# P V of the group before between the first two score chunks, row sums on DVE, odd 64 weight rows as half rows: a decode step on one Trainium2 core

## The chip, the cores and the metric

One core of one Trainium2 chip runs the whole program. The metric is the time of one execution on the device in microseconds (us), as the median of several. The profile's span, from the first to the last instruction, is about 1.8 us shorter than the time of the same execution. "Fast runs" are those not over 1.5% above the fastest of the same kernel.

PE is TensorE, which multiplies matrices and writes to PSUM; DVE (VectorE) and ACT (ScalarE) do the element-wise work; SyncE issues the loads, which 16 DMA engines carry. A load has landed when the last of the 16 engines reports it done. P is the matrix of exponentials of the scores, and "P V" its product with V.

## The reference, cut to what matters

```python
B, D, H, Sk, Dh, F = 8, 576, 32, 4096, 128, 4608          # one new token per sequence
q = (x @ wq) as [B, H, 1, Dh]
p = softmax(einsum("bhqd,bhkd->bhqk", q, k_cache) * Dh ** -0.5)
a = einsum("bhqk,bhkd->bhqd", p, v_cache) as [B, 1, H * Dh] @ wo
h = gelu(layernorm(x) @ w1 + b1);  b = h @ w2 + b2          # [576, 4608] and [4608, 576]
g = sigmoid((x * gate_w).sum(-1))
out = g * a + (1 - g) * b                                     # bfloat16
```

K and V are 268 MB each and every byte is used once, so the two caches have to stream through the core; the weights add 20 MB.

## The kernel before: the parts that matter

The work is cut into 64 groups of 4 heads of one sequence. For each group one DMA brings 4 MB of K and one brings 4 MB of V. There are two buffers for each. Within a group DVE multiplies K by q in four chunks, PE adds the products up in PSUM (8 matmuls a chunk), DVE reduces them to scores, ACT takes the exponentials, and PE multiplies P by V (32 matmuls, one group later). All DMA is issued by SyncE in program order; a V load waits for the last P V matmul that reads its buffer, a K load for the last multiply.

```python
    def load_k(g):
        s = g % 2
        nK[s] += 1
        src = kv_src(A_k_cache, g)
        k_land[g] = op("sync", lambda e: e.dma_start(KB[s][:, :, :], src), [k_done.get(g - 2)], dma=(sK[s], 16 * nK[s]))

    def load_v(g):
        s = g % 2
        nV[s] += 1
        src = kv_src(A_v_cache, g)
        t = op("sync", lambda e: e.dma_start(VB[s][:, :, :], src), [v_done.get(g - 2)], dma=(sV[s], 16 * nV[s]))
        v_land[g] = [(t, 0, NTT)]
# ... cut ...
    def pv(g, part, parts):
        s = g % 2
        for land, t0, t1 in v_land[g]:
            t0, t1 = max(t0, part * NTT // parts), min(t1, (part + 1) * NTT // parts)
            for tq in range(t0 // TQ, t1 // TQ):
                j = tq % 4
                o = o_ps[s][32 * j:32 * j + TQ * HB, :]
                w = [land, a_exp[g], a_ev.get(g - 2), *c_ps] if tq == t0 // TQ else ()
                p_pv[g] = op("tensor", lambda e, o=o, tq=tq: e.matmul(
                    o, lhsT=P[:, s, tq * TQ:(tq + 1) * TQ, :].rearrange("p t h -> p (t h)"),
                    rhs=VB[s][:, tq * TQ:(tq + 1) * TQ, :].rearrange("p t d -> p (t d)"),
                    start=(tq < 4), stop=(tq >= NTQ - 4)), w)
        v_done[g] = p_pv[g]
# ... cut ...
        def between(c, g=g):
            if g >= 1 and g < K_AHEAD:
                pv(g - 1, c, NCK)
            if c == 1:
                if g >= 2 and (g - 2) not in v_norm:
                    norm(g - 2)
                if g == UP0 + UPN:
                    act_h()
                if g == DN0 + DNN:
                    b_out()
            # ... cut: up and down projection after chunk 2 ...
        scores(g, between)          # mult 0, between(0), mult 1, between(1), reduce 0, mult 2, between(2), ...
        # ... cut ...
        if g >= K_AHEAD:            # the last two groups
            softmax(g)
            pv(g - 1, 0, 1)
        if g >= 1:
            total(g - 1)
            evict(g - 1)
            gather(g - 1)
        if g < K_AHEAD:
            softmax(g)
    # ... cut ...
    norm(NG - 2)
    pv(NG - 1, 0, 1)
    total(NG - 1)
```

`pv(g - 1, c, NCK)` is a quarter of P V after each of the four chunks. The row sums come out of the exponentials on ACT (`accum_out`). wq and w1 have 576 = 4 x 128 + 64 rows, and the last 64 rows are loaded to 64 partitions.

## Time and profile before

| what | us |
|---|---|
| time, median of the first 3 runs (range) | 1336.5 (1333.92 to 1336.59) |
| span of the profiled run | 1333.3 |
| first K load landed / last V load landed | 26.4 / 1319.5 |
| last landing to the end of the span | 13.8 |

From the page of the kernel before: busy time of the engines, two rows by 40 slices (DMA in tenths busy, and GB/s), the chain of waits, and two groups of instructions, the multiplies and the accumulator reads (count, busy us, mean ns, idle time before them and what ended it).

```profile
span 1333.3 us, 12286 instructions
...
PE 885.7 (66%) x5166; PEld 346.8 (26%) x5166; DVE 833.0 (62%) x992; ACT 205.1 (15%) x650; POOL 1.8 (0%) x10
...
DMA  9999999999999999999999999999999999999995
GB/s 379 417 411 428 415 407 419 428 417 414 432 425 420 420 422 410 415 431 419 429 431 429 431 421 431 430 428 427 431 425 434 427 428 428 432 431 428 429 432 216
...
## 4 chain that ended last, share of the span: by engine, by line
DMA 60%; PE 21%; DVE 18%; ACT 1%; issue 1%; SPq 0%; DVEq 0%
...
L330 DVE TENSOR_TENSOR p<-KB,q_bc 128x4096 bf16<-128x4096 bf16 x256 | 579.5, 2284 | 281.6 <-DMA KB<-in_A_k_cache_dram 258.9
...
L372 ACT ACTIVATION_READ_ACCUMULATOR P<-s_sb,mD 32x1 f32 x256 | 63.6, 248 | 0.0
```

The DMA row is full in every slice but the last, while no engine is over 66% busy, and the chain that ended last consists of K loads for the most part. So the stream of loads is the limit. Yet the rate is not level: in the first 19 slices it moves between 379 and 432 GB/s, from slice 21 on (but for the last) between 421 and 434.

The DMA issues of K and V: KB each, and the median time from issue to landing.

```profile
KB<-in_A_k_cache_dram SPq DMA_DIRECT2D x64, 4096.0 KB, 24.4
VB<-in_A_v_cache_dram SPq DMA_DIRECT2D x63, 4096.0 KB, 15.0
```

A load takes 9.7 us of the stream, so a K load that lands 24.4 us after its issue had one and a half loads queued before it, and a V load only about half of one. SyncE's timeline shows why (start, duration, what was issued): V and K go out together at the end of a group.

```profile
177.31 0.33 SPq L213 DMA_DIRECT2D VB<-in_A_v_cache_dram  x1
177.68 0.43 SPq L207 DMA_DIRECT2D KB<-in_A_k_cache_dram  x1
195.94 0.33 SPq L213 DMA_DIRECT2D VB<-in_A_v_cache_dram  x1
196.31 0.43 SPq L207 DMA_DIRECT2D KB<-in_A_k_cache_dram  x1
```

Three stretches of the span (us; then the stretch's length, busy time and instructions of PE, weight loads, DVE, ACT and GpSimd, the granted clock, the DMA share and GB/s): the groups with up projection, those with part of the down projection, and the rest.

```profile
100.00:320.00 220.00, 160.97 (x990) 69.09 (x990) 141.49 (x165) 33.44 (x109) 0.00 (x0) 0.80 0.99 418
340.00:520.00 180.00, 116.88 (x678) 45.72 (x679) 109.02 (x126) 25.60 (x84) 0.00 (x0) 0.77 0.99 420
560.00:1240.00 680.00, 457.01 (x2634) 172.71 (x2638) 444.37 (x516) 104.35 (x340) 0.00 (x0) 0.79 1.00 429
```

The DMA share is 0.99 to 1.00 in all three, but the rate is 418, 420 and 429 GB/s: a share near 1 does not say that the stream is at its best, because a packet that is held up counts as busy (those after the V issued at 177.31 us took 1.4 to 2.1 us instead of 1.21).

The trace has a completion count for each load and each of the 16 DMA engines. Read from these, a load of 4 MB lands 9.7 us after the one before it when nothing disturbs the stream (4.19 MB in 9.7 us is 432 GB/s).

The end of the program, from DVE's first multiply of group 62 on (timeline; start, duration, engine, line). L330 is the multiply, L340 the sums of the scores, L407 the first step of norm, L384 P V, L179 the store of the result.

```profile
1286.55 4.45 DVE L330 TENSOR_TENSOR p<-KB,q_bc 128x4096 bf16<-128x4096 bf16 x2
...
1301.98 4.45 DVE L330 TENSOR_TENSOR p<-KB,q_bc 128x4096 bf16<-128x4096 bf16 x2
...
1306.22 5.10 PE L340 MATMUL psb<-p,ident 128*128 128x512 bf16 x16
1306.40 0.18 DVE L407 RECIPROCAL rz<-psb 128x4 f32<-128x4 f32 x1
...
1323.61 3.22 PE L384 MATMUL psb<-VB,P 128*16 128x512 bf16 x32
...
1331.56 0.31 SPq L179 DMA_DIRECT2D out_dram<-out_sb  x1
```

Here every group starts as soon as the one before it is done (1286.55, 1301.98): the last groups are paced by compute, counted from the landing of K of group 61 at 1270.4 us, and not by DMA. The first multiply of group 63 stands ahead of norm(61) and does not wait for it.

### The profile page before, as it was taken

What the parts mean: (1) busy time and instruction counts of PE and PEld (TensorE: products, weight loads), DVE (VectorE), ACT (ScalarE), POOL (GpSimd) and SP (SyncE); (2) the same over time, 40 slices, a digit from 0 to 9 for tenths busy, and PEclk for the clock granted to TensorE, in tenths of its full rate; (3) what the DMA queues carried; (4) which work ended last, traced back from release to release, by engine and by line L of the source; (5) the groups of instructions that cost most, each with busy time, mean ns of one, the idle gap of its engine ahead of it and who ended that gap; (6) DMA issues with size and microseconds to landing.
All of it is one profiled execution on the core that took longest, in us unless ns stands there. A gap on an engine that the chain in (4) does not pass through costs nothing.

```text
span 1333.3 us, 12286 instructions
## 1 busy us (share of the span) xinstructions
PE 885.7 (66%) x5166; PEld 346.8 (26%) x5166; DVE 833.0 (62%) x992; ACT 205.1 (15%) x650; POOL 1.8 (0%) x10
## 2 busy tenths in 40 slices
PE   4647677677457767476676676567567667666776
PEld 1212232232122323122232222222222222222223
DVE  2637567567456765476666667667666666766774
ACT  1201110111111011001111110111111111011112
POOL 0000000000000000000000000000000000000000
PEclk9867787887678878677887787787778788868778
DMA  9999999999999999999999999999999999999995
GB/s 379 417 411 428 415 407 419 428 417 414 432 425 420 420 422 410 415 431 419 429 431 429 431 421 431 430 428 427 431 425 434 427 428 428 432 431 428 429 432 216
DMA packets 24598, 557.75 MB, mean 418 GB/s; under 512 B 2368, under 2 KB 6496, under 8 KB 6752
## 3 DMA queue, kind: packets, MB, share of 16 engines
q1 hardware_dynamic: 24368, 556.95, 98.4%
q8 instruction: 40, 0.66, 0.2%
q14 instruction: 14, 0.11, 0.0%
q10 hardware_dynamic: 176, 0.03, 0.0%
HBM read 556.96 MB, written 0.01 MB: 418 GB/s over the span
## 4 chain that ended last, share of the span: by engine, by line
DMA 60%; PE 21%; DVE 18%; ACT 1%; issue 1%; SPq 0%; DVEq 0%
DMA KB<-in_A_k_cache_dram 59%; PE psb L340 16%; DVE p L330 13%; DVE s_sb L345 4%; PE psb L384 2%; DMA RB<-in_A_wq_dram 1%; PE psb L308 1%; PE psb L419 1%; DVE mA L363 0%; ACT P L372 0%; PE psb L444 0%; PE psb L401 0%; ACT O_sb L396 0%; PE psb L465 0%; DVE mB L365 0%
## 5 line engine op out<-in xcount | busy, mean ns | idle before, releaser
L340 PE MATMUL psb<-p,ident 128*128 128x512 bf16 x2048 | 600.4, 446 | 380.7 <-DVE p L330 378.0
L330 DVE TENSOR_TENSOR p<-KB,q_bc 128x4096 bf16<-128x4096 bf16 x256 | 579.5, 2284 | 281.6 <-DMA KB<-in_A_k_cache_dram 258.9
L340 PEld LDWEIGHTS psb<-p,ident 128*128 128x128 bf16 x2048 | 203.7, 110 | 735.1 <-DVE p L330 430.8
L345 DVE TENSOR_REDUCE s_sb<-psb 128x32 f32<-128x512 f32 x256 | 176.3, 689 | 190.9 <-PE psb L340 190.4
L324 ACT ACTIVATE q_bc<-psb 128x128 bf16<-128x128 f32 x64 | 17.7, 277 | 1036.5 <-PE psb L322 1036.5
L384 PE MATMUL psb<-VB,P 128*16 128x512 bf16 x2048 | 171.0, 418 | 0.0
L372 ACT ACTIVATE P<-s_sb,mD 32x128 bf16<-32x128 f32 x256 | 147.0, 574 | 49.9 <-DVE mD L369 46.9
L401 PE MATMUL psb<-sel,O_sb 128*128 128x4 f32 x512 | 68.0, 256 | 47.7 <-ACT O_sb L396 47.7
L401 PEld LDWEIGHTS psb<-sel,O_sb 128*128 128x128 f32 x512 | 62.4, 192 | 53.3 <-ACT O_sb L396 53.3
L372 ACT ACTIVATION_READ_ACCUMULATOR P<-s_sb,mD 32x1 f32 x256 | 63.6, 248 | 0.0
L384 PEld LDWEIGHTS psb<-VB,P 128*16 128x16 bf16 x2048 | 28.9, 86 | 128.5 <-issue 127.1
L396 ACT ACTIVATE O_sb<-psb 128x512 f32<-128x512 f32 x64 | 37.9, 592 | 4.7 <-PE psb L384 4.6
L391 PE MATMUL psb<-rs,ones 128*128 128x4 f32 x128 | 21.7, 240 | 0.0
L391 PEld LDWEIGHTS psb<-rs,ones 128*128 128x128 f32 x128 | 20.0, 196 | 1.3 <-issue 1.3
L363 DVE TENSOR_REDUCE mA<-s_sb 128x1 f32<-128x128 f32 x64 | 18.3, 286 | 2.2
L308 PE MATMUL psb<-RB,p 128*8 128x512 bf16 (+1 forms) x40 | 12.7, 451 | 9.4 <-DMA RB<-in_A_wq_dram 9.4
L419 PE MATMUL psb<-yT_sb,RB 128*128 128x8 bf16 (+1 forms) x180 | 18.4, 209 | 0.0
L419 PEld LDWEIGHTS psb<-yT_sb,RB 128*128 128x128 bf16 (+1 forms) x180 | 16.4, 151 | 6.2 <-issue 5.2
L407 DVE RECIPROCAL rz<-psb 128x4 f32<-128x4 f32 x64 | 11.3, 176 | 9.0 <-PE psb L401 9.0
L369 DVE STREAM_TRANSPOSE mD<-mC 128x32 f32<-128x32 f32 x64 | 13.6, 212 | 2.2
L365 DVE STREAM_TRANSPOSE mB<-mA 128x32 f32<-128x32 f32 x64 | 13.6, 212 | 2.2
L322 PE MATMUL psb<-Q,Sel 128*128 128x128 bf16 x64 | 14.7, 229 | 0.0
(56 smaller groups left out, 99.2 us busy)
## 6 DMA issues: line engine op xcount, KB each, us to landing
KB<-in_A_k_cache_dram SPq DMA_DIRECT2D x64, 4096.0 KB, 24.4
VB<-in_A_v_cache_dram SPq DMA_DIRECT2D x63, 4096.0 KB, 15.0
RB<-in_B_w_dram SPq DMA_DIRECT2D x1, 5184.0 KB, 26.2
RB<-in_B_w_dram SPq DMA_DIRECT2D x1, 4608.0 KB, 39.6
RB<-in_A_wo_dram SPq DMA_DIRECT2D x1, 4608.0 KB, 26.9
RB<-in_A_wq_dram SPq DMA_DIRECT2D x1, 4096.0 KB, 13.1
VB<-in_A_v_cache_dram SPq DMA_DIRECT2D x1, 2048.0 KB, 12.5
VB<-in_A_v_cache_dram SPq DMA_DIRECT2D x1, 1024.0 KB, 14.7
```

What stands on the lines that cost most here:

```text
L308: p_Q = op("tensor", lambda e, o=o, r=r, kt=kt, ksz=ksz: e.matmul(o, lhsT=xT_sb[0:ksz, kt, :], rhs=r, start=(kt == 0), stop=(kt == NKT - 1 ...
L324: a_qb[g] = op("scalar", lambda e: e.activation(out=q_bc[:, g % 2, :], in_=qb_ps[:, 0:DH], func=ACT.Copy), [t, v_mult.get((g - 2, NCK - 1))])
L330: v_mult[g, c] = op("vector", lambda e: e.tensor_tensor(out=p1[:, par, :, :], in0=KB[s][:, c * CT:(c + 1) * CT, :], in1=qb, op=ALU.mult), ...
L340: p_sum[g, c] = op("tensor", lambda e, r=r, n=n: e.matmul(tr_ps[par][:, :], lhsT=ident[:, :], rhs=r, start=(n == 0), stop=(n == NCH - 1)), w)
L345: v_red[g, c] = op("vector", lambda e: e.tensor_reduce(out=s_sb[:, s, c * CT:(c + 1) * CT], in_=tr_ps[par][:, :].rearrange("p (t c) -> p t ...
L363: t = op("vector", lambda e: e.tensor_reduce(out=mA[:, 0:1], in_=s_sb[:, s, :], axis=AX.X, op=ALU.max), [v_red[g, NCK - 1], c_mA])
L372: a_exp[g] = op("scalar", lambda e, h=h, q=q: e.activation(out=P[q, s, :, h], in_=s_sb[q, s, :], func=ACT.Exp, bias=mD[q, s, 0:1], scale=1 ...
L384: p_pv[g] = op("tensor", lambda e, o=o, tq=tq: e.matmul(o, lhsT=P[:, s, tq * TQ:(tq + 1) * TQ, :].rearrange("p t h -> p (t h)"), rhs=VB[s] ...
L391: op("tensor", lambda e: e.matmul(oz_ps[:, HB:2 * HB], lhsT=ones[:, :], rhs=rs[:, g % 2, :], start=True, stop=True), [a_exp[g], v_norm.get ...
L396: a_ev[g] = op("scalar", lambda e: e.activation(out=O_sb[:].rearrange("p t d -> p (t d)"), in_=o_ps[s][:, :], func=ACT.Copy), [p_pv[g], p_ ...
L401: p_oz[g] = op("tensor", lambda e, tt=tt: e.matmul(oz_ps[:, 0:HB], lhsT=O_sb[:, tt, :], rhs=sel16[:, tt, :], start=(tt == 0), stop=(tt == ...
L419: st["p_up"] = op("tensor", lambda e, w=w, jt=jt, kt=kt, ksz=ksz: e.matmul(xy_ps[0][:, jt * B:(jt + 1) * B], lhsT=w, rhs=yT_sb[0:ksz, kt, ...
```

## The change

Its intent is to free each V buffer early, to take work off ACT, and to load the odd 64 rows of wq and w1 at the full rate. The core of the diff:

```diff
-            if g >= 1 and g < K_AHEAD:
-                pv(g - 1, c, NCK)
-            if c == 1:
-                if g >= 2 and (g - 2) not in v_norm:
-                    norm(g - 2)
+            if c == 0 and g >= 1:
+                if g < K_AHEAD:
+                    pv(g - 1, 0, 1)
+                    evict(g - 1)
+            if c == 1 and g >= 1:
+                rowsum(g - 1)
+                total(g - 1)
+            if c == 2:
+                if 1 <= g < K_AHEAD:
+                    gather(g - 1)
 ... up and down projection, cut; norm(g - 1) after chunk 3, cut ...
+        softmax(g)
         if g >= K_AHEAD:
-            softmax(g)
             pv(g - 1, 0, 1)
-        if g >= 1:
-            total(g - 1)
             evict(g - 1)
             gather(g - 1)
-        if g < K_AHEAD:
-            softmax(g)
+            norm(g - 1)
 ... cut ...
-    norm(NG - 2)
+    rowsum(NG - 1)
+    total(NG - 1)
     pv(NG - 1, 0, 1)
-    total(NG - 1)
 ... row sums ...
-                accum_out=rs[q, s, h:h + 1]), [v_nm[g], p_pv.get(g - 2), c_P, c_rs])
+    def rowsum(g):
+        s = g % 2
+        v_rs[g] = op("vector", lambda e: e.tensor_reduce(
+            out=rs[:, s, :], in_=P[:, s, :, :].rearrange("p t h -> p h t"), axis=AX.X, op=ALU.add),
+            [a_exp[g], p_z.get(g - 2)])
 ... the odd 64 rows of wq, as 128 half rows; w1 alike ...
-             load("sync", wq_sb[0:64, 4, :], A_wq[512:576, :], "ld_wqb")]
+             load("sync", wq_t, halves(A_wq), "ld_wqb")]     # w[512:576, :].rearrange("r (s n) -> (r s) n", s=2)
```

For the half rows the transposed x gets two extra blocks of columns with zeros in the rows of the other half, so all matmuls of the Q projection contract 128 rows. At the end the projection with wo runs all of output half 0 before half 1.

More of the change, by code (lines that the diff above doesn't have):

```diff
@@ L17 @@
 F = 4608
-NKT = 5
-KT_SIZES = [128, 128, 128, 128, 64]
+NKF = 4
+NKT = NKF + 1
 NJ = F // 128
@@ L117, in bass_gated_mix__mha_block_cached__mixer_channel_mlp__decode_kernel @@
     VB = [sb(f"VB{i}", [128, NTT, DH], BF16) for i in range(2)]
-    RB = sb("RB", [128, NKT * F], BF16)
-    wq_sb = view(RB, 0, [128, NKT, SK])
-    w1_sb = view(RB, 0, [128, NKT, F])
+    RB = sb("RB", [128, 9 * F // 2], BF16)
+    wq_sb = view(RB, 0, [128, 4, SK])
+    wq_t = view(RB, 4 * SK, [128, SK // 2])
+    w1_sb = view(RB, 0, [128, 4, F])
+    w1_t = view(RB, 4 * F, [128, F // 2])
     w2_sb = view(RB, 0, [128, NJ, D])
@@ L137, in bass_gated_mix__mha_block_cached__mixer_channel_mlp__decode_kernel @@
     junk = early([B, D])
-    xT_sb = early([128, NKT, B])
-    yT_sb = sb("yT_sb", [128, NKT, B], BF16)
+    xz = early([B, 2, 64, 2])
+    yz = early([B, 2, 64, 2])
+    xT_sb = early([128, NKF + 2, B])
+    yT_sb = sb("yT_sb", [128, NKF + 2, B], BF16)
     b1_sb = sb("b1_sb", [128, NJ], BF16)
@@ L191, in bass_gated_mix__mha_block_cached__mixer_channel_mlp__decode_kernel, with halves @@
     ld_b1 = load("scalar", b1_sb[:, :], B_b1.rearrange("(p j) -> p j", j=NJ), "ld_b1")
-    ld_wq = [load("sync", wq_sb[:, 0:4, :], A_wq[0:512, :].rearrange("(kt p) n -> p kt n", p=128), "ld_wqa"),
-             load("sync", wq_sb[0:64, 4, :], A_wq[512:576, :], "ld_wqb")]
+    def halves(w):
+        return w[512:576, :].rearrange("r (s n) -> (r s) n", s=2)
+    ld_wq = [load("sync", wq_sb, A_wq[0:512, :].rearrange("(kt p) n -> p kt n", p=128), "ld_wqa"),
+             load("sync", wq_t, halves(A_wq), "ld_wqb")]
     def kv_src(cache, g):
@@ L241, in bass_gated_mix__mha_block_cached__mixer_channel_mlp__decode_kernel @@
                                                   base=0, pattern=[[-1, 128]], channel_multiplier=1), [c_id0])
+    c_z = memset("gpsimd", xz, 0.0)
+    c_z = memset("gpsimd", yz, 0.0)
     c_ones = memset("gpsimd", ones[:], 1.0)
     c_mA = memset("gpsimd", mA[:], 0.0)
-    c_rs = memset("gpsimd", rs[:], 0.0)
     c_P = memset("gpsimd", P[:], 0.0)
@@ L270, in bass_gated_mix__mha_block_cached__mixer_channel_mlp__decode_kernel, with spread, transposed @@
     G_COL, OMG_COL = 9, 10
-    def transposed(src, col, waits):
+    def spread(dst, src, waits):
+        op("vector", lambda e: e.tensor_copy(out=dst[:, 0, :, 0], in_=src[:, 512:576]), [*waits, c_z])
+        return op("vector", lambda e: e.tensor_copy(out=dst[:, 1, :, 1], in_=src[:, 512:576]))
+    def transposed(src, srcz, col, waits):
         last = None
-        for kt in range(NKT):
-            ksz = KT_SIZES[kt]
-            o = xy_ps[0][0:ksz, col + kt * B:col + (kt + 1) * B]
-            i = src[0:B, kt * 128:kt * 128 + ksz]
+        for kt in range(NKF + 2):
+            o = xy_ps[0][:, col + kt * B:col + (kt + 1) * B]
+            i = src[:, kt * 128:(kt + 1) * 128] if kt < NKF else srcz[:, kt - NKF, :, :].rearrange("b r s -> b (r s)")
             last = op("tensor", lambda e, o=o, i=i: e.matmul(o, lhsT=i, rhs=ident[0:B, 0:B], start=True, stop=True),
@@ L283, in untransposed @@
     def untransposed(dst, col, waits):
-        a = op("vector", lambda e: e.tensor_copy(
-            out=dst[:, 0:4, :], in_=xy_ps[0][:, col:col + 32].rearrange("p (k b) -> p k b", k=4)), waits)
-        b = op("vector", lambda e: e.tensor_copy(out=dst[0:64, 4, :], in_=xy_ps[0][0:64, col + 32:col + 40]))
-        return a, b
-    p_xT = transposed(x_sb, 0, [ld_x, c_id])
-    _, v_xT = untransposed(xT_sb, 0, [p_xT])
+        return op("vector", lambda e: e.tensor_copy(
+            out=dst.rearrange("p k b -> p (k b)"), in_=xy_ps[0][:, col:col + (NKF + 2) * B]), waits)
+    v_xz = spread(xz, x_sb, [ld_x])
+    p_xT = transposed(x_sb, xz, 0, [ld_x, c_id, v_xz])
+    v_xT = untransposed(xT_sb, 0, [p_xT])
     t = op("vector", lambda e: e.reciprocal(out=stat[:, 7:8], in_=stat[:, 5:6]), [a_sqrt])
@@ L295, in bass_gated_mix__mha_block_cached__mixer_channel_mlp__decode_kernel @@
                                                    scalar1=-1.0, scalar2=1.0, op0=ALU.mult, op1=ALU.add), [a_g])
-    p_yT = transposed(y_sb, YT_COL, [v_y, v_xT])
-    v_yT = untransposed(yT_sb, YT_COL, [p_yT])[1]
+    v_yz = spread(yz, y_sb, [v_y])
+    p_yT = transposed(y_sb, yz, YT_COL, [v_yz, v_xT])
+    v_yT = untransposed(yT_sb[:, :, :], YT_COL, [p_yT])
     a_Q = []
@@ L303, in bass_gated_mix__mha_block_cached__mixer_channel_mlp__decode_kernel @@
             for kt in range(NKT):
-                ksz = KT_SIZES[kt]
                 o = tr_ps[half][32 * h:32 * h + B, :]
-                r = view(RB, kt * SK + half * 2048 + h * DH, [ksz, 4, DH])
-                r = bass.AP(tensor=RB, offset=r.offset, ap=[[pstride(RB), ksz], [HB * DH, 4], [1, DH]])
-                p_Q = op("tensor", lambda e, o=o, r=r, kt=kt, ksz=ksz: e.matmul(
-                    o, lhsT=xT_sb[0:ksz, kt, :], rhs=r, start=(kt == 0), stop=(kt == NKT - 1)),
+                at = (kt * SK + half * (SK // 2) if kt < NKF else NKF * SK) + h * DH
+                r = bass.AP(tensor=RB, offset=at, ap=[[pstride(RB), 128], [HB * DH, 4], [1, DH]])
+                xi = kt if kt < NKF else NKF + half
+                p_Q = op("tensor", lambda e, o=o, r=r, kt=kt, xi=xi: e.matmul(
+                    o, lhsT=xT_sb[:, xi, :], rhs=r, start=(kt == 0), stop=(kt == NKT - 1)),
                     [v_xT, *ld_wq, *c_ps] if h == kt == half == 0 else ())
@@ L312, in bass_gated_mix__mha_block_cached__mixer_channel_mlp__decode_kernel @@
             out=Q4[:, half * 512:(half + 1) * 512], in_=tr_ps[half][:, :], func=ACT.Copy, scale=inv_sqrt_dh), [p_Q]))
-    ld_w1 = [load("sync", w1_sb[:, 0:4, :], B_w1[0:512, :].rearrange("(kt p) f -> p kt f", p=128), "ld_w1a", [p_Q]),
-             load("sync", w1_sb[0:64, 4, :], B_w1[512:576, :], "ld_w1b")]
-    a_qb, v_mult, v_red, p_sum, v_nm, a_exp, p_pv, a_ev, p_oz, v_norm = ({} for _ in range(10))
+    ld_w1 = [load("sync", w1_sb, B_w1[0:512, :].rearrange("(kt p) f -> p kt f", p=128), "ld_w1a", [p_Q]),
+             load("sync", w1_t, halves(B_w1), "ld_w1b")]
+    a_qb, v_mult, v_red, p_sum, v_nm, a_exp, p_pv, a_ev, p_oz, v_norm, v_rs, p_z = ({} for _ in range(12))
     def q_of(g):
@@ L372, in softmax @@
             a_exp[g] = op("scalar", lambda e, h=h, q=q: e.activation(
-                out=P[q, s, :, h], in_=s_sb[q, s, :], func=ACT.Exp, bias=mD[q, s, 0:1], scale=1.0,
-                accum_out=rs[q, s, h:h + 1]), [v_nm[g], p_pv.get(g - 2), c_P, c_rs])
+                out=P[q, s, :, h], in_=s_sb[q, s, :], func=ACT.Exp, bias=mD[q, s, 0:1], scale=1.0),
+                [v_nm[g], p_pv.get(g - 2), v_rs.get(g - 2), c_P])
+    def rowsum(g):
[3 more added lines that the diff above has]
+            [a_exp[g], p_z.get(g - 2)])
     def pv(g, part, parts):
@@ L390, in total @@
     def total(g):
-        op("tensor", lambda e: e.matmul(oz_ps[:, HB:2 * HB], lhsT=ones[:, :], rhs=rs[:, g % 2, :], start=True, stop=True),
-           [a_exp[g], v_norm.get(g - 1), c_ones])
+        p_z[g] = op("tensor", lambda e: e.matmul(
+            oz_ps[:, HB:2 * HB], lhsT=ones[:, :], rhs=rs[:, g % 2, :], start=True, stop=True),
+            [v_rs[g], v_norm.get(g - 1), c_ones])
     def evict(g):
@@ L415, in up_proj @@
         for jt in range(j0, j1):
-            for kt in range(NKT):
-                ksz = KT_SIZES[kt]
-                w = bass.AP(tensor=RB, offset=kt * F + jt, ap=[[pstride(RB), ksz], [NJ, 128]])
-                st["p_up"] = op("tensor", lambda e, w=w, jt=jt, kt=kt, ksz=ksz: e.matmul(
-                    xy_ps[0][:, jt * B:(jt + 1) * B], lhsT=w, rhs=yT_sb[0:ksz, kt, :], start=(kt == 0),
-                    stop=(kt == NKT - 1)), [*ld_w1, v_yT] if jt == kt == 0 else ())
+            for kt in range(NKF + 2):
+                o, n, at = xy_ps[0][:, jt * B:(jt + 1) * B], 128, kt * F + jt
+                if kt >= NKF:
+                    o, n, at = xy_ps[0][64 * (kt - NKF):64 * (kt - NKF) + 64, jt * B:(jt + 1) * B], 64, NKF * F + jt
+                w = bass.AP(tensor=RB, offset=at, ap=[[pstride(RB), 128], [NJ, n]])
+                st["p_up"] = op("tensor", lambda e, w=w, o=o, kt=kt: e.matmul(
+                    o, lhsT=w, rhs=yT_sb[:, kt, :], start=(kt == 0), stop=(kt >= NKF)),
+                    [*ld_w1, v_yT] if jt == kt == 0 else ())
     def act_h():
@@ L462, in a_proj @@
     def a_proj(hg):
-        for h in range(hg * HB, (hg + 1) * HB):
-            for half in range(2):
-                st["p_a"] = op("tensor", lambda e, h=h, half=half: e.matmul(
+        for half in range(2):
+            for h in range(hg * HB, (hg + 1) * HB):
+                st["p_a"] = st["p_a", half] = op("tensor", lambda e, h=h, half=half: e.matmul(
                     xy_ps[half][0:B, 0:288], lhsT=OT_sb[:, h, :], rhs=wo_sb[:, h, half * 288:(half + 1) * 288],
@@ L490, in between @@
         def between(c, g=g):
-            if g >= 1 and g < K_AHEAD:
-                pv(g - 1, c, NCK)
-            if c == 1:
-                if g >= 2 and (g - 2) not in v_norm:
-                    norm(g - 2)
+            if c == 0 and g >= 1:
[8 more added lines that the diff above has]
+                    gather(g - 1)
+                if UP0 <= g < UP0 + UPN:
+                    up_proj((g - UP0) * NJ // UPN, (g - UP0 + 1) * NJ // UPN)
+                if DN0 <= g < DN0 + DNN:
+                    down_proj((g - DN0) * NJ // DNN, (g - DN0 + 1) * NJ // DNN)
+            if c == 3:
+                if 1 <= g < K_AHEAD:
+                    norm(g - 1)
                 if g == UP0 + UPN:
@@ L499, in between @@
                     b_out()
-            if c == 2:
-                if UP0 <= g < UP0 + UPN:
-                    up_proj((g - UP0) * NJ // UPN, (g - UP0 + 1) * NJ // UPN)
-                if DN0 <= g < DN0 + DNN:
-                    down_proj((g - DN0) * NJ // DNN, (g - DN0 + 1) * NJ // DNN)
         scores(g, between)
@@ L512, in bass_gated_mix__mha_block_cached__mixer_channel_mlp__decode_kernel @@
             load_wo()
+        softmax(g)
         if g >= K_AHEAD:
-            softmax(g)
             pv(g - 1, 0, 1)
-        if g >= 1:
-            total(g - 1)
             evict(g - 1)
             gather(g - 1)
-        if g < K_AHEAD:
-            softmax(g)
-        if g >= AP0 and (done_a + 1) * B < g:
+            norm(g - 1)
+        if g >= AP0 and (done_a + 1) * B <= g:
             a_proj(done_a)
             done_a += 1
-    norm(NG - 2)
+    rowsum(NG - 1)
+    total(NG - 1)
     pv(NG - 1, 0, 1)
-    total(NG - 1)
     evict(NG - 1)
@@ L538, in bass_gated_mix__mha_block_cached__mixer_channel_mlp__decode_kernel @@
             out=out_sb[:, q], in0=xy_ps[half][0:B, 0:288], scalar=stat[:, G_COL:G_COL + 1], in1=bmg_sb[:, q],
-            op0=ALU.mult, op1=ALU.add), [st["p_a"], st["v_bmg"], a_g]))
+            op0=ALU.mult, op1=ALU.add), [st["p_a", half], st["v_bmg"], a_g]))
     ld_out = load("sync", out_flat, out_sb[:, :], "ld_out", last)
```

## The prediction

> **What bounds the kernel now.** The DMA stream. In the page's slices DMA is at 9 tenths throughout, 418 GB/s over the span; PE is 66% and DVE 62% busy, and the chain of waits gives the K loads 59%. In the trace's completion counts a 4 MB K or V load lands 9.7 us after its predecessor whenever the stream is undisturbed (432 GB/s, beside the 435 GB/s fabric ceiling in the Trainium skill, "DMA: Bandwidth & Descriptors", Specifications). From the first K landing (26.4 us) to the last V landing (1319.5 us) the loads would need 127 x 9.71 us plus about 38 us for w1, w2 and wo; they take about 21 us more.
>
> Where those go: P V of group g-1 is spread over all four chunks, so V is issued at the end of a group, together with the next K (timeline of SyncE: V at 177.31, K at 177.68). By then only one K load is left in the queue, with 3 to 5 us to run, and the 16 engines drift apart by 2 to 3 us. The packets show the early engines idle for 1 to 4 us around 138, 178 and 219 us, and the packets after that take 1.4 to 2.1 us instead of 1.21. In 100 to 320 us (groups with up projection) this costs about 7 us; in quiet groups after 640 us almost nothing.
>
> **What the change does.**
> 1. V is released after P V in chunk 0: about 9 us after K landed instead of 14 to 17. The lowest backlog rises from about 4 us to over 10. Starvation should vanish. The instruction fetches (40 packets of 16 KB, each holding up one engine by about 1.4 us) stay, about 6 us on the slowest engine. Gain: 14 us, estimated.
> 2. 64-row packets run at half rate: 8 KB took 0.63 us against 0.31, 9 KB 0.71 against 0.35. As 128 half rows wq saves 1.25 us and w1 1.4 us of the stream. Gain: 2.6 us.
> 3. Row sums leave ACT (accumulator reads, 64 us busy, off the path) and go to DVE: about 0.65 us a group, like the 0.69 us reduce of the same size. P V in one burst (about 2.7 us) delays chunk 1 on PE. A group's DVE chain grows from about 16 to 18 us (estimate), still under 19.4 us of DMA, so it costs nothing until the end.
> 4. The end is paced by compute from K of group 61 on (1270.4 us): 16, 15.4, 16, then 15 us. There I expect a loss: group 61 carries the burst (+1.7 us); norm(61) now stands before the first multiply of group 63 on DVE and waits for exp, evict and gather (+1.8); row sums and total stand before the last P V (+1), exps are shorter (-1), output half 0 overlaps the projection of half 1 (-0.4). Net +3.
>
> **Sum:** -14 - 2.6 + 3 = about -14 us: 1322 us. Range 1313 to 1329. Faster by over 2%: 0.05, within 2%: 0.94, slower: 0.01.
>
> **What would show it.** V issued about 6 us ahead of K in SyncE's timeline; landings 9.7 us apart nearly everywhere, GB/s near 430 in the slices at 100 to 560 us; last V landing near 1303 us; last landing to end 15 to 18 us instead of 14; less DVE idle time before the multiplies.
>
> **What would make it wrong.** If slow packets come from HBM or the rings and not from starvation, the gain is a few us. If up-projection groups exceed 19.4 us of compute[...], compute bounds them and about 5 us of the gain go. The same if the slowest engine's fetches add up to more.

## The result, and the profile after

| | before | after |
|---|---|---|
| time, median us (range, runs) | 1336.55 (1333.92 to 1337.55, 4) | 1323.88 (1322.61 to 1325.94, 4) |
| span of the profiled run | 1333.3 | 1321.4 |
| last V load landed | 1319.5 | 1304.1 |
| last landing to the end | 13.8 | 17.3 |
| K and V landings more than 0.1 us late, of 126 | 28, by 19.4 us | 10, by 8.0 us |

(Where exactly the line is drawn moves such counts by a few landings, and the sums by under 1 us.) The ratio is 0.991, with a 95% interval of 0.989 to 0.9929. Ratios here are the mean time of one kernel's fast runs over that of the other's of the same rounds, so not quite the ratio of the medians quoted. In three later sets of rounds the kernel before had medians of 1331.88 (11 runs, 1328.95 to 1338.9), 1331.62 (11 runs) and 1334.11 us (9 runs), so its first runs were among its slower ones; in the last of these sets the kernel after had 1324.49 us and a ratio of 0.9927 (0.9908 to 0.9946). The run of the kernel after that was profiled in that set (after_again, 1326.04 us) landed its last V at 1303.8 us, like the first, but took 20.5 us from there to the end instead of 17.3: the end of this kernel differs by some 3 us between executions.

The page of the kernel after, the same parts as before (its L343 is the multiply, L391 the row sum on DVE):

```profile
span 1321.4 us, 12174 instructions
...
PE 834.4 (63%) x5204; PEld 376.9 (29%) x5204; DVE 873.5 (66%) x1058; ACT 211.2 (16%) x394; POOL 2.3 (0%) x11
...
DMA  9999999999999999999999999999999999999993
GB/s 398 428 429 428 429 434 430 434 429 427 434 431 430 435 428 422 422 435 430 430 431 430 430 433 430 431 431 429 429 436 430 431 430 430 430 432 435 405 430 159
...
## 4 chain that ended last, share of the span: by engine, by line
DMA 63%; PE 22%; DVE 14%; ACT 0%; issue 0%; SPq 0%
...
L343 DVE TENSOR_TENSOR p<-KB,q_bc 128x4096 bf16<-128x4096 bf16 x256 | 579.4, 2284 | 190.8 <-DMA KB<-in_A_k_cache_dram 190.8
...
L391 DVE TENSOR_REDUCE rs<-P 128x4 f32<-128x512 bf16 x64 | 43.4, 679 | 0.0
```

In slices 2 to 15 the rate is now 427 GB/s or more, where it was 407 to 432 before, the multiplies wait 190.8 us for K instead of 258.9, DVE is up from 62% to 66% with 43.4 us of row sums, and the accumulator reads on ACT are gone.

The issues of K and V:

```profile
KB<-in_A_k_cache_dram SPq DMA_DIRECT2D x64, 4096.0 KB, 26.1
VB<-in_A_v_cache_dram SPq DMA_DIRECT2D x63, 4096.0 KB, 21.1
```

V now has 21.1 us from issue to landing instead of 15.0, so 6.1 us more were queued ahead of it. SyncE's timeline in two groups with up projection:

```profile
163.62 0.33 SPq L221 DMA_DIRECT2D VB<-in_A_v_cache_dram  x1
168.37 0.33 SPq L215 DMA_DIRECT2D KB<-in_A_k_cache_dram  x1
183.15 0.33 SPq L221 DMA_DIRECT2D VB<-in_A_v_cache_dram  x1
187.88 0.33 SPq L215 DMA_DIRECT2D KB<-in_A_k_cache_dram  x1
```

V goes out 4.7 us ahead of K. The three stretches:

```profile
100.00:320.00 220.00, 162.57 (x1063) 78.04 (x1060) 151.84 (x180) 34.90 (x66) 0.00 (x0) 0.81 1.00 431
340.00:520.00 180.00, 119.02 (x747) 53.98 (x747) 122.47 (x145) 28.54 (x54) 0.00 (x0) 0.83 1.00 431
560.00:1240.00 680.00, 431.86 (x2646) 190.71 (x2645) 469.68 (x559) 110.39 (x210) 0.00 (x0) 0.82 1.00 431
```

431 GB/s in each. The end, the same events as before:

```profile
1270.88 4.45 DVE L343 TENSOR_TENSOR p<-KB,q_bc 128x4096 bf16<-128x4096 bf16 x2
...
1290.55 0.18 DVE L427 RECIPROCAL rz<-psb 128x4 f32<-128x4 f32 x1 [4.95 <-PE psb L421]
...
1290.84 4.49 DVE L343 TENSOR_TENSOR p<-KB,q_bc 128x4096 bf16<-128x4096 bf16 x2
...
1293.19 5.97 PE L353 MATMUL psb<-p,ident 128*128 128x512 bf16 x16 [2.68 <-DVE p L343]
...
1310.88 0.68 DVE L391 TENSOR_REDUCE rs<-P 128x4 f32<-128x512 bf16 x1
...
1312.13 3.32 PE L403 MATMUL psb<-VB,P 128*16 128x512 bf16 x32
...
1319.66 0.31 SPq L183 DMA_DIRECT2D out_dram<-out_sb  x1
```

DVE's multiply of group 63 now starts only at 1290.84, right after norm(61) (1290.55), which had to wait for the gather; in the kernel before it started 15.4 us after that of group 62, now 20.0 us. The last P V waits for the row sum (1310.88).

### The profile page after: what moved, and what is told of

Same layout as the page of the kernel before. It is cut to its first block, busy times and chain, and to the rows that moved or that the text cites. A ratio compares the mean times of both kernels' runs of the same rounds, so it can differ in the third digit from the quotient of the medians.

```text
span 1321.4 us, 12174 instructions
## 1 busy us (share of the span) xinstructions
PE 834.4 (63%) x5204; PEld 376.9 (29%) x5204; DVE 873.5 (66%) x1058; ACT 211.2 (16%) x394; POOL 2.3 (0%) x11
## 4 chain that ended last, share of the span: by engine, by line
DMA 63%; PE 22%; DVE 14%; ACT 0%; issue 0%; SPq 0%
DMA KB<-in_A_k_cache_dram 63%; PE psb L353 15%; DVE p L343 11%; PE psb L403 6%; DVE s_sb L358 2%; PE psb L421 0%; ACT P L385 0%; PE psb L441 0%; ACT O_sb L416 0%; DVE mA L376 0%; PE psb L487 0%; DVE rz L427 0%; DVE mB L378 0%; SPq L183 0%; DVE gm L379 0%
## 5 line engine op out<-in xcount | busy, mean ns | idle before, releaser
L343 DVE TENSOR_TENSOR p<-KB,q_bc 128x4096 bf16<-128x4096 bf16 x256 | 579.4, 2284 | 190.8 <-DMA KB<-in_A_k_cache_dram 190.8
L353 PEld LDWEIGHTS psb<-p,ident 128*128 128x128 bf16 x2048 | 208.1, 111 | 765.2 <-DVE p L343 490.6
L403 PE MATMUL psb<-VB,P 128*16 128x512 bf16 x2048 | 150.1, 445 | 0.0
L403 PEld LDWEIGHTS psb<-VB,P 128*16 128x16 bf16 x2048 | 49.7, 100 | 116.2 <-issue 88.0
L421 PEld LDWEIGHTS psb<-sel,O_sb 128*128 128x128 f32 x512 | 67.8, 194 | 17.5 <-ACT O_sb L416 8.7
L421 PE MATMUL psb<-sel,O_sb 128*128 128x4 f32 x512 | 62.0, 244 | 7.0 <-ACT O_sb L416 7.0
L391 DVE TENSOR_REDUCE rs<-P 128x4 f32<-128x512 bf16 x64 | 43.4, 679 | 0.0
L410 PEld LDWEIGHTS psb<-rs,ones 128*128 128x128 f32 x128 | 24.4, 192 | 10.2 <-DVE rs L391 1.2
L427 DVE RECIPROCAL rz<-psb 128x4 f32<-128x4 f32 x64 | 11.3, 176 | 14.8 <-PE psb L421 14.8
L410 PE MATMUL psb<-rs,ones 128*128 128x4 f32 x128 | 18.3, 213 | 1.1 <-DVE rs L391 1.1
L335 PE MATMUL psb<-Q,Sel 128*128 128x128 bf16 x64 | 14.3, 224 | 0.0
L379 DVE TENSOR_REDUCE gm<-mB 128x1 f32<-128x32 f32 x64 | 11.9, 186 | 2.2
## 6 DMA issues: line engine op xcount, KB each, us to landing
VB<-in_A_v_cache_dram SPq DMA_DIRECT2D x63, 4096.0 KB, 21.1
```

The costliest lines, as they stand in the source:

```text
L343: v_mult[g, c] = op("vector", lambda e: e.tensor_tensor(out=p1[:, par, :, :], in0=KB[s][:, c * CT:(c + 1) * CT, :], in1=qb, op=ALU.mult), ...
L353: p_sum[g, c] = op("tensor", lambda e, r=r, n=n: e.matmul(tr_ps[par][:, :], lhsT=ident[:, :], rhs=r, start=(n == 0), stop=(n == NCH - 1)), w)
L391: v_rs[g] = op("vector", lambda e: e.tensor_reduce(out=rs[:, s, :], in_=P[:, s, :, :].rearrange("p t h -> p h t"), axis=AX.X, op=ALU.add), ...
L403: p_pv[g] = op("tensor", lambda e, o=o, tq=tq: e.matmul(o, lhsT=P[:, s, tq * TQ:(tq + 1) * TQ, :].rearrange("p t h -> p (t h)"), rhs=VB[s] ...
L410: p_z[g] = op("tensor", lambda e: e.matmul(oz_ps[:, HB:2 * HB], lhsT=ones[:, :], rhs=rs[:, g % 2, :], start=True, stop=True), [v_rs[g], v_ ...
L421: p_oz[g] = op("tensor", lambda e, tt=tt: e.matmul(oz_ps[:, 0:HB], lhsT=O_sb[:, tt, :], rhs=sel16[:, tt, :], start=(tt == 0), stop=(tt == ...
```

## The experiments

All kernels here gave the reference's result within tolerance. The theory: the gain comes from the DMA queue no longer running dry, because V is queued earlier; the end, which is paced by compute, gives part of it back. The rivals: (A) the half rows with their faster Q projection, (B) the row sums leaving ACT, (C) P V in one burst instead of four pieces, wherever it stands. A fourth, (D), needs no run of its own: the mean granted clock of TensorE was 0.79 to 0.80 in the runs of the kernel before and 0.81 in those of the kernel after. But b_pv_c1 was as fast at 0.78 to 0.79, and b_pv_c3 the slowest at 0.81 to 0.82, so the clock did not make the gain.

Two figures are used for all of them, worked out from SyncE's timeline and the completion counts: how long after the landing of a group's K load the next V load was issued, and the margin, which is the time from that issue to the moment at which the first of the 16 engines reports the last queued load (the next K) as done. (The prediction's "backlog" counts to the last engine instead, 2.4 to 2.9 us later in the kernel before.) Medians for the stretches 85 to 320, 340 to 540 and 560 to 1240 us.

| kernel | time, us | ratio to before, same rounds (95%) | V issued after K landed | margin | last V landed | late K, V landings |
|---|---|---|---|---|---|---|
| before | 1331.6 to 1336.6 (four medians) | 1 | 15.5, 15.3, 14.3 | 1.7, 1.8, 2.6 | 1319.5 | 28, 19.4 us |
| after | 1323.88 | 0.991 (0.989 to 0.9929) | 8.4, 8.3, 8.2 | 9.2, 8.1, 5.1 | 1304.1 | 10, 8.0 us |
| b_early_pv | 1324.06 | 0.9931 (0.9908 to 0.9954) | 8.2, 8.3, 8.2 | 8.4, 7.1, 4.4 | 1307.2 | 10, 6.9 us |
| b_pv_c1 | 1324.62 | 0.9926 (0.9908 to 0.9944) | 10.0, 9.9, 10.1 | 5.8, 4.4, 4.0 | 1308.2 | 4, 6.4 us |
| b_pv_c2 | 1325.12 | 0.9933 (0.9912 to 0.9953) | 12.7, 12.7, 12.7 | 4.0, 3.1, 2.8 | 1306.7 | 6, 6.3 us |
| b_pv_c3 | 1351.1 | 1.0127 (1.0099 to 1.0154) | 15.9, 16.1, 15.5 | 1.8, 1.9, 2.1 | 1336.3 | 46, 36.1 us |
| b_half_rows | 1331.72 | 0.9984 (0.996 to 1.0009) | 16.0, 15.2, 14.3 | 1.6, 2.2, 2.7 | 1316.1 | 26, 20.3 us |
| b_v_halves | 1328.52 | 0.9959 (0.9933 to 0.9984) | first half 6.2, 6.2, 4.9 us ahead of the second | not comparable | 1312.6 | not comparable |
| a_norm_late | 1322.27 | 0.9924 (0.991 to 0.9938) | 8.7, 8.4, 8.1 | 8.8, 7.8, 5.2 | 1304.1 | 13, 8.0 us |
| a_pv_first | 1323.7 | 0.9936 (0.9923 to 0.9948) | 8.6, 8.4, 8.3 | 8.7, 7.5, 5.1 | 1304.1 | 15, 8.3 us |
| a_act_sums | 1323.23 | 0.9935 (0.9923 to 0.9947) | 8.8, 8.2, 8.2 | 8.7, 7.9, 5.6 | 1302.9 | 6, 5.8 us |
| a_tail | 1318.23 | 0.9898 (0.9883 to 0.9913) | 8.4, 8.1, 8.2 | 8.9, 8.0, 5.5 | 1303.9 | 10, 7.7 us |

### The early P V alone: b_early_pv

```diff
-            if g >= 1 and g < K_AHEAD:
-                pv(g - 1, c, NCK)
+            if c == 0 and g >= 1 and g < K_AHEAD:
+                pv(g - 1, 0, 1)
```

> The kernel before with one thing changed: all of P V of group g-1 stands in one burst after chunk 0 of group g; row sums, 64-row loads, evict, gather, norm and the last groups stay as they were. Theory (starved DMA queue): this alone carries the gain. V is issued 5 to 6 us ahead of K, landings 9.7 us apart, the last V lands near 1306 us instead of 1319.5, the end is paced as before, so about 1323 us (1320 to 1326), 12 to 14 us under the kernel before. Rival A (half rows and the faster Q projection made the gain): about 1335. Rival B (taking the accumulator reads off ACT made it): about 1336.

Measured: 1324.06 us (1322.91 to 1326.1, 6 runs). The stretches, with the rate in the last column:

```profile
100.00:320.00 220.00, 154.01 (x994) 75.45 (x995) 145.80 (x167) 35.35 (x113) 0.00 (x0) 0.80 1.00 431
340.00:520.00 180.00, 121.06 (x742) 53.39 (x743) 115.54 (x132) 25.30 (x82) 0.00 (x0) 0.81 1.00 431
560.00:1240.00 680.00, 446.08 (x2677) 191.49 (x2675) 448.59 (x525) 107.40 (x350) 0.00 (x0) 0.82 1.00 431
```

This edit alone brings the rate to 431 GB/s everywhere and the time to that of the kernel after. Rivals A and B fall: neither the half rows nor the row sums are in this kernel. The time is the one expected, the gain is not: between the medians of these rounds it is 7.8 us, where 12 to 14 were expected, because the kernel before ran at 1331.88 us here and at 1335.12 us in the profiled run from which the estimate was made.

### The same burst, late: b_pv_c3

```diff
-            if g >= 1 and g < K_AHEAD:
-                pv(g - 1, c, NCK)
+            if c == 3 and g >= 1 and g < K_AHEAD:
+                pv(g - 1, 0, 1)
```

> The kernel before with the same one burst of P V, but after chunk 3 instead of chunk 0, so that V is released no earlier than before. Theory (starved queue): V goes out at the end of the group, a little later than before, so nothing is gained: 1335 to 1341 us, last V landing 1318 to 1324. Rival C (it is the burst, that is P V no longer breaking into the score chunks on PE, and not the time at which V is issued): about 1324 us as with the early burst.

Measured: 1351.1 us (1345.32 to 1354.29, 6 runs). Rival C falls, and by more than expected: the kernel is 1.3% slower than before. The stretches:

```profile
100.00:320.00 220.00, 155.12 (x987) 74.93 (x986) 141.08 (x165) 32.67 (x108) 0.00 (x0) 0.82 0.99 415
340.00:520.00 180.00, 116.97 (x685) 51.08 (x678) 107.78 (x126) 28.93 (x91) 0.00 (x0) 0.78 0.99 420
560.00:1240.00 680.00, 440.71 (x2587) 186.93 (x2591) 435.40 (x507) 101.36 (x330) 0.00 (x0) 0.81 1.00 422
```

The quiet stretch, 560 to 1240 us, falls from 429 to 422 GB/s. There the kernel before issued V 14.3 us after K landed and was just on the safe side; the burst issues it 15.5 us after, and 46 landings come late. The 10 us by which the expectation was missed are this stretch, which I had taken for safe. Compute did not become the limit: DVE still sat idle for 3.4 us or more before the first multiply of each of groups 3 to 61, until K had landed.

### How early is early enough: b_pv_c1 and b_pv_c2

The same edit with `c == 1` and `c == 2`.

> The kernel before with the burst of P V after chunk 1. Theory (starved queue): V goes out about 10.5 us after K landed, with 3 us or more before the first engine runs dry, where the early burst had 3.1 at the least; landings stay 9.7 us apart and the time is that of the early burst, 1323 to 1327 us. If the gain grew evenly with the earliness of V, between 1324 (after chunk 0) and 1351 (after chunk 3): about 1333 us.

> The kernel before with the burst of P V after chunk 2. Theory (starved queue): V goes out about 13 us after K landed, the first engine then has 2 to 4 us left, on the edge; part of the groups starve: 1325 to 1333 us, under the kernel before or level with it. If the gain grew evenly with earliness: about 1342 us.

Measured: 1324.62 us (1323.67 to 1325.31, 5 runs) and 1325.12 us (1323.53 to 1326.22, 5 runs). The four positions of the burst give 1324, 1325, 1325 and 1351 us. So the time does not grow evenly with the delay of V; there is an edge, and the starving that was expected in part of the groups of b_pv_c2 did not come. With a median margin of 2.8 us or more the stream ran undisturbed, with 2.1 us or less it did not, and the kernel before stood at 1.7 to 2.6 us. Group by group the edge is a slope: counted over before, after, b_early_pv, b_half_rows, b_pv_c1, b_pv_c2 and b_pv_c3 between 85 and 1240 us, V and the K behind it came more than 0.1 us late together in 23 of 26 groups with a margin under 1.5 us, in 44 of 88 with 1.5 to 2.5 us, and in 43 of 287 with more. That also fits its scatter: its runs spread over 10 us, those of the kernels with a wider margin over 2 to 5 us; the cause of the scatter was not tested by itself.

### More in the queue with P V left where it was: b_v_halves

```diff
-        t = op("sync", lambda e: e.dma_start(VB[s][:, :, :], src), [v_done.get(g - 2)], dma=(sV[s], 16 * nV[s]))
+        t = op("sync", lambda e: e.dma_start(VB[s][:, 0:64, :], src[:, 0:64, :]), [v_half.get(g - 2)], dma=(sV[s], 16 * nV[s]))
+        u = op("sync", lambda e: e.dma_start(VB[s][:, 64:128, :], src[:, 64:128, :]), [v_done.get(g - 2)], dma=(sV2[s], 16 * nV[s]))
 ... in pv ...
+                if tq == NTQ // 2 - 1:
+                    v_half[g] = p_pv[g]
```

> The kernel before with P V spread over the chunks as before; only the V load is split in two halves of 2 MB, each with its own semaphore, and the first half waits only for the P V matmuls that read it (chunks 0 and 1). So half a V load is queued about 4 us earlier and nothing is moved on PE, DVE or ACT. Theory (starved queue): the lowest backlog rises by about 4.9 us and most of the starvation goes: 1323 to 1328 us. If the place of P V on PE matters and not the queue: 1336 us, or more for the extra DMA.

Measured: 1328.52 us (1326.82 to 1330.48, 6 runs), just past the upper end of what was expected. No instruction of PE, DVE or ACT was moved, and the kernel is faster than before (interval 0.9933 to 0.9984), which the fuller queue explains. One thing else changed: V now comes in packets of 16 KB instead of 32 KB. That alone does not make the undisturbed stream faster (below), but no run separates it from the earlier issue where the stream is disturbed. Between 100 and 320 us the packets show 0.5 us of gaps and 0.3 us of lengthened packets per DMA engine in the mean, against 3.2 and 4.3 us in the kernel before (worked out by chaining each engine's packets by start and duration). Where the rest of the gain went is shown too: in the undisturbed stream one K and one V load together took 19.43 us in b_early_pv and 19.51 us here (medians), so the split costs 0.08 us of stream each time. The smaller packets account for it: two of 16 KB took 2 x 613 ns where one of 32 KB took 1215 ns (medians of this trace), and of a V load each engine carries eight of the latter, which makes 0.09 us. Over 63 groups that is 5 us (worked out), and the last V landed 5.4 us later than in b_early_pv.

### The half rows alone: b_half_rows

The kernel before with the diff's changes of wq and w1, their loads, transposes and matmuls, and nothing else.

```diff
-             load("sync", wq_sb[0:64, 4, :], A_wq[512:576, :], "ld_wqb")]
+             load("sync", wq_t, halves(A_wq), "ld_wqb")]
 ... w1 alike; two zero-filled half blocks of x and of layernorm(x) transposed; all matmuls over 128 rows ...
```

> The kernel before with the half rows of wq and w1 alone. Theory: the two 64-row loads shorten by 1.2 and 1.4 us of stream, the Q projection falls from 12.7 us to about 4.4 us but is off the path because K of group 2 is not needed until 80 us; starvation later stays. About 1334 us, 2 to 3 us under the kernel before, perhaps less if the starved groups give it back. Rival A (half rows and the Q projection carry the gain): 1324 to 1328 us.

Measured: 1331.72 us (1328.9 to 1334.18, 6 runs), a ratio of 0.9984 with 1 inside the interval. The mechanism is there: the second wq load landed 1.3 us after the first instead of 2.4, the second w1 load 1.4 instead of 2.8, and the last V load landed 3.4 us earlier in the profiled run. Between b_early_pv and the kernel after, which differ by the half rows, the row sums and the end, the last V landing moves by 3.1 us. But as a time by itself it is not distinguishable in a kernel that scatters by 10 us. The Q projection in the kernel before (PE's timeline):

```profile
16.87 12.72 PE L308 MATMUL psb<-RB,p 128*8 128x512 bf16 x40 [9.42 <-DMA RB<-in_A_wq_dram]
```

And in the kernel after:

```profile
15.13 4.35 PE L321 MATMUL psb<-RB,p 128*8 128x512 bf16 x40 [6.71 <-DMA RB<-in_A_wq_dram]
```

It falls from 12.7 to 4.4 us with the same 40 matmuls, and took 5.4 us in b_half_rows. This is off the path, as expected: w1 is queued behind V of group 1 anyway.

### The end: a_norm_late, a_pv_first, a_act_sums

Three edits of the kernel after: norm(61) back in group 63 behind its second multiply; the last P V ahead of its row sum and total; row sums back on ACT.

```diff
 # a_norm_late
-            norm(g - 1)                       # last two groups, after gather
+                if g >= 2 and (g - 2) not in v_norm:
+                    norm(g - 2)               # after chunk 1
 # a_pv_first
+    pv(NG - 1, 0, 1)
     rowsum(NG - 1)
     total(NG - 1)
-    pv(NG - 1, 0, 1)
 # a_act_sums
+                accum_out=rs[q, s, h:h + 1]), ...          # in the exponentials; rowsum() issues nothing
```

> The kernel after, with norm of group 61 put back to where the kernel before had it (in group 63, after its second multiply). Theory (the end is paced by compute and norm(61) ahead of the first multiply of group 63 on DVE costs about 4.4 us there, of which PE would have lost some anyway): 2 to 4 us faster than after, about 1320 to 1322 us, with the first multiply of group 63 starting right after softmax(62). If the end is paced by the last V load: no change, 1324 us.

> The kernel after, with P V of the last group ahead of its row sum and total on PE. Theory: the last P V starts about 1.0 to 1.5 us earlier because it need not wait for norm(62), the row sum and the total, so 1 us faster than after: about 1323 us. If it were free: no change.

> The kernel after, with the row sums put back on ACT as accumulator reads of the exponentials, nothing on DVE. Theory: in the middle both fit under the DMA stream, so nothing; at the end the total no longer waits for a row sum on DVE (0.7 us) and the exponentials take the same 2.33 us, so 0.5 to 1.5 us faster than after: about 1323 us. Rival B (moving row sums off ACT made the gain): about 1336 us.

Measured: 1322.27 us (1318.83 to 1323.56, 6 runs), 1323.7 us (1322.05 to 1323.92, 5 runs) and 1323.23 us (1322.58 to 1323.71, 5 runs), beside 1323.88 and 1324.49 us of the kernel after in two other sets of rounds. By these medians a_norm_late is faster by 1.6 to 2.2 us, at or just short of the 2 us that were expected at the least, but its interval overlaps that of the kernel after, and its profiled run (span 1321.7) lies between the two of the kernel after (1321.4 and 1324.2). PE began the sums of group 63 at 1291.72 us, there at 1293.19 and 1293.47; the last gather and the last P V took 1.87 and 3.59 us, as in after_again, but 1.06 and 3.32 us in the first profile of the kernel after. So a gain is likely and not proven. The other two differ from the kernel after by no more than its two medians do from each other, so their effect, expected at about 1 us, stays unproven. What a_act_sums does show: rival B falls once more (with the row sums on ACT it is as fast), and the row sums on DVE cost about 1 us at most before the end (its last V landed at 1302.9 us, those of the kernel after at 1304.1 and 1303.8).

### A version with the end rearranged: a_tail, a_tail_again, after_again

```diff
             if c == 2:
+                if g >= K_AHEAD:
+                    pv(g - 1, 0, 1)
+                    evict(g - 1)
             if c == 3:
+                if g >= K_AHEAD:
+                    gather(g - 1)
 ... after softmax(g), for the last two groups ...
-            pv(g - 1, 0, 1)
-            evict(g - 1)
-            gather(g - 1)
             norm(g - 1)
 ... after the last group ...
+    pv(NG - 1, 0, 1)
     rowsum(NG - 1)
     total(NG - 1)
-    pv(NG - 1, 0, 1)
```

> A version meant to beat both: the kernel after with the end rearranged. In groups 62 and 63 P V of the group before and its evict stand after chunk 2, gather after chunk 3, norm after softmax, and the last P V stands ahead of its row sum and total. Theory (the end is paced by compute from K of group 61 on): 4 to 7 us faster than after, about 1318 us, last landing to end about 12 us instead of 17. If the last V load paces the end: at most 1 us.

> The rearranged end again, beside the kernel after in the same rounds. Expected 1318 us, 5 to 6 us under the kernel after of these rounds; were the earlier difference one of rounds, no difference.

> The kernel after, unchanged, in more rounds: the kernel before scattered from 1329 to 1339 us in the last two sets of rounds (median 1332) against 1334 to 1338 in the first four runs, so the gain has to be taken again. Expected: after at 1324 us with little scatter as all three kernels without starvation showed, the kernel before 1329 to 1339, so a ratio of 0.991 to 0.995.

Measured: 1318.23 us (1316.25 to 1318.35, 4 runs), ratio 0.9898; in the second set 1319.11 us (1316.5 to 1319.77, 4 runs), ratio 0.9882 (0.986 to 0.9904), beside after_again with 1324.49 us (1322.87 to 1326.04, 5 runs), ratio 0.9927 in the same rounds. So the end is worth 5.4 us between the medians of the same rounds. Its timeline from the multiply of group 63 on:

```profile
1286.64 4.49 DVE L343 TENSOR_TENSOR p<-KB,q_bc 128x4096 bf16<-128x4096 bf16 x2
...
1296.98 1.90 PE L403 MATMUL psb<-VB,P 128*16 128x512 bf16 x32
...
1305.21 3.58 PE L403 MATMUL psb<-VB,P 128*16 128x512 bf16 x32 [3.70 <-ACT P L385]
...
1312.73 0.31 SPq L183 DMA_DIRECT2D out_dram<-out_sb  x1
```

P V of group 62 (1296.98) now runs inside group 63, and the multiply of group 63 starts 4.2 us earlier than in the kernel after, though K of group 61 landed within 0.2 us of the same time (1254.2 against 1254.4). Last landing to end: 10.6 us (10.7 in a_tail_again) instead of 17.3 and 20.5. Now the last P V starts 1.3 us after the last V landing (1303.9), so compute and the stream end nearly together.

## Why the prediction was right

**The bound and its mechanism: right.** Early release of V alone makes the gain (b_early_pv), a fuller queue without moving any compute makes part of it (b_v_halves), and the same burst placed late loses (b_pv_c3). The prediction named the queue running dry with 3 to 5 us left, and over 10 us after the change. Counted to the last engine, as it did, it was 4.0, 4.8 and 5.2 us before (medians of the three stretches) and 11.2, 11.4 and 11.3 us after. Counted to the first engine, which is the one that runs dry, it was 1.7 to 2.6 us before, and the edge lies between 2.1 and 2.8 us.

**Gain 1, 14 us: right in its mechanism, too high in size.** The last V landing moved from 1319.5 to 1307.2 us with the early burst, 12.3 us, measured from an execution of 1335.12 us, above the medians of all later rounds; between the medians of the same rounds the gain was 7.8 us. The fetches stayed (40 packets before, 41 after), and that they are what still comes late is argued and not tested: 8.0 us of late landings remain in the kernel after, estimated at 6; 1.0 us of these is K of group 62 at 1265.1 us: there SyncE's order puts K of group 62 ahead of V of group 61, so both went out at the end of group 60 as before the change.

**Gain 2, 2.6 us: right as a change of the stream, 3.1 to 3.4 us in the last V landing; as a time by itself not proven.**

**Row sums and burst cost nothing in the middle: right in result, not in its reason.** DVE's chain of a group grew from 15.6 us (the group at 1016 us before) to 17.0 us (the one at 1001 us after). The burst made that and not the row sums: over groups 25 to 60 the median was 15.6 us before, 16.9 us in b_early_pv and in after 16.8 us. In groups with up projection it was 18.2 us (174.75 to 192.93), but "still under 19.4 us of DMA" failed for 4 of these 12: groups 5, 8, 11 and 12 took 20.0 to 20.3 us, and the first multiply of groups 6, 9 and 12 began 0.5 to 0.8 us after K had landed (five such groups and up to 1.55 us in after_again; none over 17.9 us in b_early_pv). What was feared, compute over 19.4 us, did happen. It cost nothing in the stream, which kept 431 GB/s there: groups 6, 9 and 13 were shorter again (17.2 to 17.3 us), and the margin was 8 to 10 us.

**The end, +3 us: near in sum by luck, wrong in its terms.** From the landing of K of group 61 to the end of the span it took 62.9 us before (1270.4 to 1333.3) and 67.0 us after (1254.4 to 1321.4), +4.1. Piece by piece, from the timelines: K of group 61 to the first multiply of group 62, 16.2 to 16.5 us, +0.3 where "group 61 carries the burst (+1.7 us)" was said. From there to the first sums of group 63 on PE, 19.7 to 22.3 us, +2.6 where norm(61) was put at 1.8; DVE lost 4.5 us there, but PE, which before had to finish the gather first, only part of it. From there to the last P V, 17.4 to 18.9 us, +1.6 where +1 - 1 was said. From the last P V to the end, 9.7 to 9.3 us, -0.4 as said, but 11.0 us in after_again, so this term is not shown. The step that failed is "exps are shorter (-1)": four exponentials took 2.36 us with the accumulator reads (1302.09 to 1304.45) and 2.33 us without (1285.63 to 1287.96), because each read lay within the time of the exponential before it. The sum depends on the execution, too: in after_again the same way took 70.0 us, and 63.7 to 64.0 us in b_early_pv, b_pv_c1, b_pv_c2 and b_half_rows, which end like the kernel before. So the end cost 3 to 7 us.

**The time: 1322 us said, 1323.88 us measured.** In the profiled runs the sum is -16.0 us (landing of K of group 61) + 4.1 us = -11.9 us, against -16.6 + 3 said. That it fits so well is in part luck: the terms of the end missed by up to 1.6 us each, and in the other profiled execution of the kernel after the end took 3 us more.

The Trainium skill, "DMA: Bandwidth & Descriptors", Specifications, gives 435 GB/s as the fabric ceiling; the undisturbed stream here ran at 431 to 432 GB/s, so it agrees. The skill's "SBUF — State Buffer", Door 1: the DMA port swizzle, says that partitions 0 to 63 reach only 8 of the 16 ports; the trace agrees, 0.63 us for an 8 KB packet to 64 partitions against 0.31 us. "TensorEngine Tiling (Array Packing)", Key Properties, says that changing the tiling mode drains TensorE; the Q projection, which changed between 128 and 64 rows every fifth matmul, is compatible with it (12.7 against 4.4 to 5.4 us). But the starts of its matmuls show two things: before, they follow one another, later on 0.21 to 0.22 us apart and 0.31 us before and after one over 64 rows, so the switches themselves account for about 1.4 to 2 us (an estimate from 15 such steps of 0.09 to 0.13 us); the larger part is that after the change matmuls of different heads overlap (starts at 15.51, 15.52, 15.90, 15.90 and 15.94 us). No run isolated the drain, and whether it kept them from overlapping is open; the up projection before, with the same alternation, shows none: 15 matmuls took 1.56 us there, 18 without 64-row ones 1.67 us after.

## What to carry to other kernels

When DMA shows full in every slice, compare its rate in different stretches: a queue that runs dry for a microsecond in each group shows as a lower rate and hardly as an idle share (here 418 against 431 GB/s, at shares of 0.99 and 1.00). What counts is how much work is queued when the next load is issued, and it has an edge: once the margin is safely past it, freeing the buffer still earlier gains nothing, and close to it a delay of about one microsecond (b_pv_c3) cost 1.3%. When the stream is fixed, look at the end, where compute sets the pace: moving the same instructions there gained 5 us more.

## What the Trainium skill lacked or had wrong

- "DMA: Bandwidth & Descriptors" has no figure for how much must still be queued when the next load is issued. Here 2.8 us or more to the first engine's completion (medians) kept the stream undisturbed, 2.1 us or less did not (b_pv_c2, b_pv_c3); a V issued at 177.31 us had its first packets at 178.29 us, and those took 1.4 to 2.1 us instead of 1.21.
- The same page (Anatomy of one DMA, which is about the SWDGE path) puts the fixed cost of a DMA down to completion latency; it has no figure for what splitting a 4 MB load costs a full queue issued by SyncE. Here it was 0.08 us of stream, which the packets of 16 KB instead of 32 KB account for (b_v_halves).
- The same page's Specifications gives about 358 GB/s, half of a stack, as the HBM limit of a core; that is, as the page says further down, the share with both cores streaming, and no bound for one alone: with one core running, the stream here held 431 to 432 GB/s.
- "Runtime: NRT & Kernel Launch", Instruction fetch mechanics, calls the cost of crossing a 16 KB block mostly hidden, and means the sequencer. From a stream bound by DMA the fetch takes time: 40 to 41 such packets in a run, and the one at 153.1 us held one engine up by 0.87 us and lengthened its next packet by 0.55 us.
- "ScalarE: Activation LUTs" mentions the accumulator output without its cost; here four reads with their exponentials took 2.36 us, the exponentials alone 2.33 us.
- "TensorEngine Tiling (Array Packing)" has no figure for the drain at a change of tiling mode; here matmuls of the Q projection started 0.31 us apart around one over 64 rows and 0.21 to 0.22 us apart elsewhere (later heads of the kernel before).
